# Scores by parity of the head on quarter-size products, one turn of the probabilities per parity, and other duration numbers in the planner of an attention, FFT and feed-forward kernel

## The chip, the cores and the metric

The kernel runs on one core of a Trainium2 chip, in one launch. The metric is device time in microseconds (us), from the first instruction to the last with what lies around them; the median of the runs is compared. Engine names are those of the profile: PE is TensorE (matrix products, with PEld for its weight loads), DVE is VectorE, ACT is ScalarE, POOL is GpSimd, SP is SyncE, whose queue issues the transfers.

## What is computed

Sliding-window attention (8 batches, 8 heads, 576 tokens, head size 64, each query sees itself and the 63 keys before it), whose output is mixed by a two-dimensional FFT, added back, normalized and sent through a two-layer feed-forward network of width 2048.

```python
def _attn_ref(q, k, v):
    scores = scale * np.matmul(q, k.transpose(0, 1, 3, 2))
    mask = (rel >= 0) & (rel < window)            # rel = query - key, window = 64
    scores = np.where(mask, scores, -1000000000.0)
    ...
    return np.matmul(attn, v)

def _moe_ref(x, w_ch1, w_ch2):
    X = np.fft.fft(np.fft.fft(x, axis=1), axis=2)
    u = x + np.real(X)
    un = (u - mu) / np.sqrt(var + 1e-06)
    return u + np.maximum(un @ w_ch1, 0.0) @ w_ch2
```

## The kernel before

**Tiles and stages.** The 4608 tokens are 36 tiles of 128 (T = 0 to 35); two batches make 9 tiles. `attn_tile(T)` loads k, q and v, turns k and q so that the head size lies on the partitions, makes scores, masks and exponentiates them, turns the probabilities, multiplies with v and normalizes into `xu`. `fft(b)` mixes a batch (products `pg`, then `pz`), `norm_tile` adds and normalizes, `ffn(c)` runs the feed-forward network on a chunk of two tiles: for each of 16 slices f twelve products of 256 columns into `ph` (L1207), a relu in two parts (ACT L1222, then DVE L1225) and six products of 512 columns into `po` (L1188). Chunk 0 is done in f32, all others in pairs of f16 parts (high and low), three products for one.

**Two kinds of attention tile.** Tiles below `PRO` = 13 are plain: f32, turned by PE through PSUM and copied out. From 13 on tiles are split: an ACT cast makes the high part, POOL or DVE subtracts it for the low part, and the turn is a transposing DMA on SP's queue: one for k (L487), two for q (L499), four for the probabilities (L626), one for the FFT's input in most tiles (L765), one for the normalized input of the feed-forward network (L1050).

**Scores before.** A tile's 128 queries are worked in two halves of 64, called jj. In a plain tile q is copied by two ACT or DVE copies into a zeroed, block-diagonal layout (`qbd`), so that one 128x128 product (L568) makes the scores of a pair of heads for one half: four products per half, eight per tile. In a split tile a half takes 16 products with 64 columns of weights (L575). Partitions of a score tile `psc` are (parity of the head, 64 queries). Since an output tile `pa` of the product with v (L657) holds four heads for both halves, both of its parts read the turned probabilities of both halves.

**What sets the order.** Nothing runs in the order of the code. Every step is an `op` with an engine (or two to choose from), a duration, a latency, a priority and the buffers it reads and writes; `Plan.order` simulates engines and rings of buffers and emits the instructions in the order found, each engine's queue in that order. PE, DVE, ACT, POOL and SP each work their queue strictly in that order. Feed-forward products have priority numbers over 1e6, so they fill what attention and FFT leave free. An op that may go to two engines goes to the second when that would be done earlier by more than a margin. `SEM` is added to a result that another engine reads, `SELF` to one that the same engine reads, `FIXED` to every duration; `TURN` and `HTURN` are the time that a transposing DMA holds SP's queue. Where the planner sees a gap on PE before the feed-forward network starts, `warm` products fill it.

**Rings.** `pr` (scores and probabilities) and `pt` (turned probabilities) have two buffers, PSUM ring `ps` four, `xu` ten: the first product with v of tile T takes the `xu` buffer that tile T - 10 leaves.

## Time and profile before

| | |
|---|---|
| median of 3 runs | 1018.03 us (1016.69 to 1024.65) |
| span of the profiled execution | 1015.3 us |
| PE busy | 972.7 us, 96% of the span |
| DVE, ACT, POOL busy | 679.6, 417.9, 197.4 us |
| granted TensorE clock, mean | 0.993 |

Busy time is the union of the engine's instructions. Matmuls are pipelined, so a busy PE is not PE at its peak. In rows with a bracket, the bracket holds the idle time before the instruction and what ended it. A queue's own rows (SPq) show how long issuing took, not the transfer.

### The profile page before, as it was taken

The page shows a single profiled execution, that of the slowest core. Times are in us where ns is not written, and L with a number is a line of the kernel's source. Part 1 is how long each engine was busy: PE and PEld are TensorE (multiplying, and loading weights), DVE is VectorE, ACT ScalarE, POOL GpSimd, SP SyncE. Part 2 cuts the span into 40 slices and gives each one's busy share as a digit, 9 for nine tenths or more (in the row PEclk, how much of TensorE's full clock was granted, in tenths as well). Part 3 has the DMA queues.
Part 4 walks back from the last instruction along what each step waited for, and adds up shares of the span by engine and source line. Part 5 has one row for each costly group of instructions (what it writes and reads, how often), then busy time and mean ns, then how long its engine had stood idle before and what let it go on. Part 6 is the DMA issues. An engine that isn't in the chain of part 4 may idle for free.

```text
span 1015.3 us, 22449 instructions
## 1 busy us (share of the span) xinstructions
PE 972.7 (96%) x8756; PEld 687.3 (68%) x8756; DVE 679.6 (67%) x1979; ACT 417.9 (41%) x1047; POOL 197.4 (19%) x203
## 2 busy tenths in 40 slices
PE   8889989999999989998999999999999999999998
PEld 7677757676676657665676666766676667676665
DVE  5899899888777767565787769676686636441121
ACT  6666656744554335323354335333453213121111
POOL 1000100042244223332022302233021300220000
PEclk9999999999999999999999999999999999999999
DMA  8987673235989866878668766867565421230000
GB/s 194 244 224 198 191 188 109 71 78 94 160 152 178 160 114 143 142 137 141 126 111 172 144 126 108 173 131 161 89 111 108 94 38 37 60 74 21 1 22 21
DMA packets 310538, 123.06 MB, mean 121 GB/s; under 512 B 292568, under 2 KB 292696, under 8 KB 310432
## 3 DMA queue, kind: packets, MB, share of 16 engines
q1 hardware_dynamic: 307712, 112.71, 54.8%
q0 software_dynamic: 2720, 8.92, 3.3%
q8 instruction: 69, 1.13, 0.5%
q14 instruction: 37, 0.30, 0.1%
HBM read 54.97 MB, written 14.17 MB: 68 GB/s over the span
## 4 chain that ended last, share of the span: by engine, by line
PE 75%; DVE 8%; DMA 8%; SPq 5%; ACT 2%; issue 2%; POOL 0%; DVEq 0%; ACTq 0%; POOLq 0%
PE ph L1207 30%; PE po L1188 30%; PE pz L924 3%; PE pa L657 3%; DMA pt<-flex 2%; DMA kn<-in_k 2%; PE pg L890 2%; PE psc L568 2%; PE psc L575 2%; SPq L626 2%; SPq L499 1%; DVE y L691 1%; PE pp L606 1%; SPq L427 1%; DVE pr L587 1%
## 5 line engine op out<-in xcount | busy, mean ns | idle before, releaser
L1207 PE MATMUL ph<-uhl,w0s 128*128 128x256 f16 (+1 forms) x3384 | 427.1, 277 | 10.1 <-DVE hh L1225 10.1
L1188 PE MATMUL po<-w1s,hh 128*128 128x512 f16 (+1 forms) x1696 | 428.1, 389 | 0.0
L1207 PEld LDWEIGHTS <-w0s 128*128 128x128 f16 x3264 | 318.0, 98 | 97.6 <-issue 14.5
L1225 DVE SCALAR_TENSOR_TENSOR hh<-ph,hh 128x256 f16<-128x256 f32 x272 | 114.5, 422 | 231.7 <-ACT hh L1222 225.8
L1222 ACT ACTIVATE hh<-ph 128x256 f16<-128x256 f32 x272 | 103.6, 382 | 392.9 <-PE ph L1207 297.1
L1188 PEld LDWEIGHTS <-hh 128*128 128x128 f16 x1632 | 157.0, 98 | 138.8 <-issue 1.9
L595 ACT ACTIVATE pr<-pr,nm 128x128 f32<-128x128 f32 x288 | 90.9, 392 | 13.2 <-DVE nm L587 13.1
L587 DVE CUSTOM_DVE_ANT_0 pr<-psc,mskb 128x128 f32<-128x128 f32 x288 | 65.5, 285 | 15.3 <-PE psc L568 11.3
L1045 POOL TENSOR_TENSOR up<-un,up 128x512 f16<-128x512 f32 x33 | 39.7, 1204 | 75.8 <-ACT up L403 73.1
L620 POOL TENSOR_TENSOR flex<-pr,flex 128x512 f16<-128x512 f32 x23 | 27.4, 1190 | 133.8 <-ACT flex L403 93.5
L1022 POOL TENSOR_TENSOR rs<-mv,mhalf 128x1 f32<-128x1 f32 x36 | 21.0, 584 | 157.9 <-DVE mv L1018 152.2
L484 POOL TENSOR_TENSOR flex<-kn,flex 128x512 f16<-128x512 f32 x19 | 25.0, 1314 | 125.0 <-ACT flex L403 119.3
L998 POOL DMA_INDIRECT mt<-md,gix x34 | 36.5, 1073 | 57.4 <-DMA md<-mp 48.8
L657 PE MATMUL pa<-va,pt 128*64 128x65 f16 (+1 forms) x760 | 39.3, 205 | 7.5 <-DMA pt<-flex 7.5
L657 PE MATMUL pa<-ve,pt 128*64 128x65 f16 (+1 forms) x760 | 39.4, 205 | 0.3 <-DMA ve<-va 0.3
L403 ACT CAST flex<-pr 128x512 f16<-128x512 f32 x39 | 24.0, 615 | 23.5 <-DMA pt<-flex 21.1
L691 DVE TENSOR_TENSOR y<-xu 128x256 f32<-128x256 f32 x68 | 32.1, 512 | 0.6
L669 DVE TENSOR_TENSOR xu<-pa,rc 128x256 f32<-128x256 f32 x72 | 30.6, 425 | 2.6
L568 PE MATMUL psc<-kst,qbd 128*128 128x128 f32 x208 | 28.2, 282 | 3.1 <-ACT qbd L403 1.2
L924 PE MATMUL pz<-g,ds__75 97*96 97x257 f16 (+3 forms) x240 | 29.3, 273 | 1.4 <-DVE g L900 1.4
L657 PEld LDWEIGHTS <-pt 128*64 128x64 f16 x1104 | 20.7, 113 | 14.7 <-DMA pt<-flex 7.9
L495 POOL TENSOR_TENSOR flex<-qn,flex 128x1024 f16<-128x1024 f32 x12 | 26.2, 2187 | 16.3 <-ACT flex L403 14.1
(155 smaller groups left out, 1108.0 us busy)
## 6 DMA issues: line engine op xcount, KB each, us to landing
wd<-in_moe_w_ch SPq DMA_DIRECT2D x20, 512.0 KB
out<-xu SPq DMA_DIRECT2D x36, 256.0 KB
ve<-va SPq DMA_DIRECT2D x67, 130.0 KB
kn<-in_k SPq DMA_DIRECT2D x32, 256.0 KB
qn<-in_q SPq DMA_DIRECT2D x32, 256.0 KB
flex<-in_moe_w_ch SPq DMA_DIRECT2D x12, 512.0 KB
flex<-in_v SPq DMA_DIRECT2D x20, 256.0 KB
md<-mp SPq DMA_DIRECT2D x24, 192.0 KB
```

The lines of the kernel that those rows point to most:

```text
L568: nc.tensor.matmul(p_[:, hp], qw, keys(hp, jj), start=True, stop=True)
L587: nc.vector.tensor_tensor_reduce(out=t["pr", jj][:, hp], in0=t["ps", jj][:, hp], in1=mskb[:, m : m + P], scale=-0.125, scalar=3.0e38, op0= ...
L595: nc.scalar.activation(pr, pr, AF.Exp, bias=t["nm", jj][:, hp : hp + 1], scale=-1.0)
L657: nc.tensor.matmul(pa[64 * jj : 64 * jj + 64, hh], pt[:, sl], v_, start=(x == 0), stop=(x == len(mm) - 1))
L691: eng.tensor_tensor(out=o, in0=p0, in1=p1, op=al)
L924: nc.tensor.matmul(pz[:M, c0:c1], ds_[:NJ, a, c[0] : c[0] + c[1]], t["g", gi][:, b_, c0:c1], start=(x == 0), stop=(x == len(mm) - 1),)
L998: nc.gpsimd.indirect_dma_start(out=mts[T], out_offset=None, in_=mds[pb][0 : HR if n < 4 else 2 * HR], in_offset=bass.IndirectOffsetOnAxis( ...
L1045: eng.tensor_tensor(out=t["up"][:, 1], in0=t["un"], in1=t["up"][:, 0], op=ALU.subtract)
L1188: nc.tensor.matmul(t["po"][i], l_, r_, start=(f == 0 and x == 0), stop=(f == NKF - 1 and x == len(mm) - 1))
L1207: nc.tensor.matmul(ph, l_, r_, start=(x == 0), stop=(x == len(mm) - 1))
L1222: nc.scalar.activation(t["hh", f][:, 0], ph, AF.Relu)
L1225: nc.vector.scalar_tensor_tensor(out=hh[:, 1], in0=ph, scalar=0.0, in1=hh[:, 0], op0=ALU.max, op1=ALU.subtract)
```

## The change

1. **Parity in place of halves.** A score tile now holds the heads of one parity g for all 128 queries of the tile: partitions are (half jj, 64 queries). The mask table grows from 320 to 384 columns (three variants of 128). The four heads of parity g, both halves, need only the turned probabilities of that parity, so each of the two products with v waits for one `pt` tile.
2. **Plain tiles: 64x64 products.** q is copied as it lies (one copy of 128x512 in place of two of 64x512), the zeroing of `qbuf` on POOL goes, and scores are 16 products with 64 rows and 64 columns of weights: rows by parity, columns by half, written to two PSUM banks. One op of 1.6 in the planner (`WSC`) in place of two of 0.95; it takes both `pr` buffers at once.
3. **Split tiles: one turn per parity.** Two transposing DMAs of 128 partitions in place of four of 64. The number and size of the products is as before.
4. **The planner's numbers.** `FIXED` falls to 0 (it was 0.1 on DVE and ACT, 0.06 on POOL), `SEM` and `SELF` rise by as much; `TURN` rises from 1.26 to 1.5 and replaces `HTURN` (1.2) for the probabilities, whose latency goes from 1.8 to 2.2.

```diff
-TURN = 1.26
-HTURN = 1.2
+TURN = 1.5
+WSC = 1.6
-    SEM = {"PE": 0.22, "DVE": 0.06, "ACT": 0.06, "POOL": 0.08, "DMA": 0.0}
+    SEM = {"PE": 0.22, "DVE": 0.16, "ACT": 0.16, "POOL": 0.14, "DMA": 0.0}
-    SELF = {"PE": 0.05, "DVE": 0.02, "ACT": 0.02, "POOL": 0.03, "DMA": 0.0}
-    FIXED = {"PE": 0.0, "DVE": 0.1, "ACT": 0.1, "POOL": 0.06, "DMA": 0.0}
+    SELF = {"PE": 0.05, "DVE": 0.12, "ACT": 0.12, "POOL": 0.09, "DMA": 0.0}
+    FIXED = {"PE": 0.0, "DVE": 0.0, "ACT": 0.0, "POOL": 0.0, "DMA": 0.0}
...
-        op("POOL", 1.0, -498 + i, lambda i=i: nc.gpsimd.memset(qbuf[i], 0.0), writes=[Bq[i]])
...
-            for h in range(2):
-                op("ACT", 0.48, base + 0.6, lambda e, h=h: q_copy(h, e), [bpq], [Bq[i]], alt=("DVE", 0.6), port=False)
+            op("ACT", 0.48, base + 0.6, lambda e: copy(e, q32[i], t["pq"]), [bpq], [Bq[i]], alt=("DVE", 0.6), port=False)
...
-                for hp in range(4 if whole else 0):
-                    qw = qbd32[i][:, hp, jj].rearrange("p h s -> p (h s)")
-                    nc.tensor.matmul(p_[:, hp], qw, keys(hp, jj), start=True, stop=True)
...
+        def score(groups):
+            for g in groups:
+                t["pr", g] = sb([P, 4, P], F32, "pr", f"pr{T}_{g}")
+                t["ps", g] = bank("ps", f"psc{T}_{g}")
+            for hp in range(4):
+                for z in range(1 if whole else 2):
+                    for g in groups:
+                        for jj in range(2):
+                            out = t["ps", g][64 * jj : 64 * jj + 64, hp]
+                            if whole:
+                                rows = slice(64 * g, 64 * g + 64)
+                                nc.tensor.matmul(
+                                    out, q32[i][rows, hp, 64 * jj : 64 * jj + 64], keys(hp, jj, rows), start=True, stop=True
+                                )
...
+        if whole:
+            op("PE", WSC, base + 2, lambda: score((0, 1)), rd, [*bss, *bps])
...
-            op("DMA", HTURN, base + 4.2 + jj, lambda g=p_turn: g(0), [bpp], [bt, bt2], lat=1.8)
-            op("DMA", HTURN, base + 4.3 + jj, lambda g=p_turn: g(1), [bpp], [bt2], lat=1.8)
+            op("DMA", TURN, base + 4.2 + g, p_turn, [bpp], [bt], lat=2.2)
...
-            rd = [*bpt[0], *bpt[1], Bve[i], Bva[i]]
+            rd = [*bpt[g], Bve[i], Bva[i]]
```

**Where instructions move.** On SP's queue around the probabilities of tile 24 (`pt24`), a place in the middle of the program, there stood before (`kst` is the turn of k, `qbd` that of q, `py` that of the FFT's input, `kn` and `flex` from `in_v` are loads):

```order
L487 DMA_TRANSPOSE kst_79<-flex_78 128x8x128
L427 DMA qn28_7349<-in_q 128x8x64
L765 DMA_TRANSPOSE py23_7371<-yp23_7299 128x8x128
L626 DMA_TRANSPOSE pt24_0_7398<-flex_78 128x8x64
L540 DMA ve1_83<-va1_81 64x520
L952 DMA md2_7448<-mp4_1_7336 96x512
L427 DMA flex_78<-in_v 128x8x64
L626 DMA_TRANSPOSE pt24_0_7398<-flex_78 128x8x64
L626 DMA_TRANSPOSE pt24_1_7489<-flex_78 128x8x64
L952 DMA md2_7448<-mp4_2_7357 96x512
L499 DMA_TRANSPOSE qbd1_77<-flex_78 128x16x64
L626 DMA_TRANSPOSE pt24_1_7489<-flex_78 128x8x64
```

and now at the same place:

```order
L482 DMA_TRANSPOSE kst_79<-flex_78 128x8x128
L756 DMA_TRANSPOSE py23_7284<-yp23_7269 128x8x128
L626 DMA_TRANSPOSE pt24_0_7307<-flex_78 128x8x128
L535 DMA ve1_83<-va1_81 64x520
L427 DMA flex_78<-in_v 128x8x64
L943 DMA md2_7385<-mp4_1_7288 96x512
L626 DMA_TRANSPOSE pt24_1_7388<-flex_78 128x8x128
L494 DMA_TRANSPOSE qbd1_77<-flex_78 128x16x64
```

Two of the four issues are gone, and the load of q of tile 28 no longer stands ahead. Over the whole program 92 such transposes become 46; all other transfers keep their number.

On PE the products with v of tile 22 (`pa22`) stood behind the 256-column products of chunk 7, slice 8:

```order
L1207 MATMUL ph7_8_6830<-uhl7_5935,w0s_84 128x256
L657 LDWEIGHTS pt22_0_6770
L657 MATMUL pa22_0_6908<-ve0_82,pt22_0_6770 64x65
L657 LDWEIGHTS pt22_1_6826
L657 MATMUL pa22_0_6908<-va0_80,pt22_1_6826 64x65
```

and their first part stands now behind the 512-column products of chunk 7, slice 0:

```order
L1179 MATMUL po7_1_6885<-w1s_85,hh7_0_6731 128x512
L650 LDWEIGHTS pt22_0_6695
L650 MATMUL pa22_0_6902<-ve0_82,pt22_0_6695 64x65
L650 LDWEIGHTS pt22_0_6695
L650 MATMUL pa22_0_6902<-va0_80,pt22_0_6695 64x65
```

The part reads one `pt` tile now, and stands five and a half slices of the feed-forward network earlier. Counted in 256-column products of that network already issued (a 512-column product as two), the first product with v of a split tile stands 111 earlier in the mean of the 23 tiles, from 216 earlier (tile 32) to 96 later (tile 34).

On POOL the rows from the normalization of tile 10 (`rs10`, `mt` is a gather) to the low part of k of tile 20 were, before (`up` is the low part of a normalized tile, `flex` that of k, q or the probabilities `pr`):

```order
L1022 TENSOR_TENSOR rs10_4289<-mv10_4244,mhalf_70 128x1
L998 DMA mt11_4302<-md1_3878,gix_73 128x512
L484 TENSOR_TENSOR flex_78<-kn19_4210,flex_78 128x8x64
L1022 TENSOR_TENSOR rs11_4402<-mv11_4363,mhalf_70 128x1
L998 DMA mt12_4406<-md1_3878,gix_73 128x512
L1045 TENSOR_TENSOR up10_4409<-un10_4331,up10_4409 128x512
L495 TENSOR_TENSOR flex_78<-qn18_4103,flex_78 128x8x128
L1045 TENSOR_TENSOR up11_4495<-un11_4423,up11_4495 128x512
L1022 TENSOR_TENSOR rs12_4525<-mv12_4491,mhalf_70 128x1
L1045 TENSOR_TENSOR up12_4587<-un12_4529,up12_4587 128x512
L484 TENSOR_TENSOR flex_78<-kn20_4538,flex_78 128x8x64
```

and are now:

```order
L1013 TENSOR_TENSOR rs10_4220<-mv10_4200,mhalf_70 128x1
L989 DMA mt11_4247<-md1_3802,gix_73 128x512
L621 TENSOR_TENSOR flex_78<-pr16_1_3867,flex_78 128x4x128
L1013 TENSOR_TENSOR rs11_4366<-mv11_4310,mhalf_70 128x1
L989 DMA mt12_4373<-md1_3802,gix_73 128x512
L1013 TENSOR_TENSOR rs12_4451<-mv12_4425,mhalf_70 128x1
L1036 TENSOR_TENSOR up12_4530<-un12_4454,up12_4530 128x512
L621 TENSOR_TENSOR flex_78<-pr17_1_4313,flex_78 128x4x128
L479 TENSOR_TENSOR flex_78<-kn20_4608,flex_78 128x8x64
```

The low parts of the normalized tiles 10 and 11 and of q of tile 18 are no longer on POOL's queue. What left POOL runs on DVE. Over the program POOL loses 18 of 33 low parts `up`, 6 of 19 of k, 5 of 12 of q, 4 of 23 of the probabilities, 6 of 7 sums of the FFT's input (L718) and one of its folds; DVE takes all of them, and a net 6 casts and scalings of ACT more.

## Rows read from the trace of the kernel before

**Rows 1.** The answer on cores and clock: span of the profiled execution and mean granted TensorE clock.

```profile
core 0: 1015.3 us, clock 0.993
```

**Rows 2.** The table of stretches, one row for each (us from the start): length, then busy time of each engine with its count of instructions in brackets, granted clock as a share, DMA share and GB/s.

```profile
0.00:86.00 86.00, 73.28 (x716) 59.73 (x717) 68.18 (x259) 55.16 (x143) 7.13 (x20) 0.98 0.90 222
86.00:171.00 85.00, 80.15 (x514) 59.13 (x513) 77.52 (x218) 49.46 (x132) 5.64 (x6) 0.98 0.65 175
171.00:800.00 629.00, 607.78 (x5982) 424.46 (x5980) 458.36 (x1326) 273.37 (x671) 164.35 (x155) 0.99 0.69 129
800.00:1015.30 215.30, 211.48 (x1550) 144.02 (x1548) 75.54 (x181) 39.94 (x103) 20.27 (x22) 1.00 0.15 35
```

**Rows 3.** The timeline of PE near the end, where only the feed-forward network is left: start, duration, engine, line, operation, how many.

```profile
999.63 1.47 PE L1207 MATMUL ph<-uhl,w0s 128*128 128x256 f16 x12
...
1002.24 1.47 PE L1207 MATMUL ph<-uhl,w0s 128*128 128x256 f16 x12
```

**Rows 4.** The list of PE's waits over the whole span: what waited, for what, then total us, times, longest.

```profile
PE ph L1207 <- DVE hh L1225: 10.1, 10, 2.8
PE pa L657 <- DMA pt<-flex: 7.5, 4, 3.8
PE ph L1207 <- DVE wf L1111: 3.7, 1, 3.7
```

**Rows 5.** The timeline of all engines around the longest wait of the start.

```profile
149.16 0.73 DVE L1111 SCALAR_TENSOR_TENSOR wf<-flex,wf 128x512 uint16<-128x512 uint32 x1
...
149.95 0.93 PE L1207 MATMUL ph<-uhl,wf 128*128 128x256 f32 x2 [3.67 <-DVE wf L1111]
```

**Rows 6.** The table of stretches again, for two short ones; the last but two of the columns is the granted clock.

```profile
365.00:370.00 5.00, 4.15 (x55) 2.71 (x56) 4.33 (x12) 1.25 (x2) 3.18 (x2) 0.66 0.33 53
467.00:472.00 5.00, 5.00 (x27) 2.93 (x25) 1.67 (x4) 0.38 (x1) 0.00 (x0) 0.66 0.96 194
```

**Rows 7.** SP's issuing by source line: how many, then shortest, median and longest in ns.

```profile
L626 SPq DMA_TRANSPOSE pt<-flex x92: 1193/1264/2272, 254.4 to 820.9; - x92
...
L487 SPq DMA_TRANSPOSE kst<-flex x23: 1231/1316/2780, 156.3 to 735.2; - x23
```

**Rows 8.** The timeline of all engines around the longest of PE's waits for turned probabilities.

```profile
356.05 2.60 SPq L626 DMA_TRANSPOSE pt<-flex  x2
...
360.06 1.14 SPq L427 DMA_DIRECT2D kn<-in_k  x1
...
361.25 1.32 SPq L626 DMA_TRANSPOSE pt<-flex  x1
...
365.85 0.26 PE L657 MATMUL pa<-va,pt 128*64 128x65 f16 x1 [3.76 <-DMA pt<-flex]
```

**Rows 9.** The timeline of all engines around the longest of PE's waits for the relu.

```profile
458.64 2.12 POOL L495 TENSOR_TENSOR flex<-qn,flex 128x1024 f16<-128x1024 f32 x1 [2.20 <-DVE flex L407]
...
459.22 2.10 DVE L620 TENSOR_TENSOR flex<-pr,flex 128x512 f16<-128x512 f32 x1 [0.67 <-ACT flex L403]
...
466.29 0.42 DVE L1225 SCALAR_TENSOR_TENSOR hh<-ph,hh 128x256 f16<-128x256 f32 x1
...
466.76 1.84 PE L1207 MATMUL ph<-uhl,w0s 128*128 128x256 f16 x12 [2.79 <-DVE hh L1225]
```

**Rows 10.** The groups of DVE by line over the span: busy us, mean ns of one, idle before.

```profile
L691 DVE TENSOR_TENSOR y<-xu 128x256 f32<-128x256 f32 x68 | 32.1, 512 | 0.6
...
L758 DVE SCALAR_TENSOR_TENSOR yp<-y,yp 128x512 f16<-128x512 f32 x17 | 14.9, 877 | 0.3
...
L495 DVE TENSOR_TENSOR flex<-qn,flex 128x1024 f16<-128x1024 f32 x11 | 13.4, 1220 | 1.1 <-DMA py<-yp 0.5 <-ACT flex L403 0.5
```

**Rows 11.** DVE by source line: shortest, median and longest in ns of the same operations and of the low parts of the probabilities.

```profile
L691 DVE TENSOR_TENSOR y<-xu x68: 408/419/1390, 17.1 to 830.3; 128x256 f32<-128x256 f32 x68
...
L758 DVE SCALAR_TENSOR_TENSOR yp<-y,yp x17: 676/683/2496, 294.5 to 814.5; 128x512 f16<-128x512 f32 x17
...
L620 DVE TENSOR_TENSOR flex<-pr,flex x23: 679/691/2097, 252.3 to 792.7; 128x512 f16<-128x512 f32 x23
```

**Rows 12.** The groups of POOL between 171 and 800 us: busy us, mean ns of one.

```profile
L1045 POOL TENSOR_TENSOR up<-un,up 128x512 f16<-128x512 f32 x25 | 30.5, 1222 | 64.4 <-ACT up L403 63.5 <-DVE up L407 0.8
...
L495 POOL TENSOR_TENSOR flex<-qn,flex 128x1024 f16<-128x1024 f32 x12 | 26.2, 2187 | 16.3 <-ACT flex L403 14.1 <-DVE flex L407 2.2
...
L484 POOL TENSOR_TENSOR flex<-kn,flex 128x512 f16<-128x512 f32 x18 | 23.5, 1306 | 102.6 <-ACT flex L403 96.9 <-DVE flex L407 5.5
```

**Rows 13.** The timeline of PE in a plain tile: all scores of a tile, after the last products with v of the tile before (f32; each product leaves two records).

```profile
29.04 0.22 PE L657 MATMUL pa<-ve,pt 128*64 128x65 f32 x1
29.04 0.22 PE L657 MATMUL pa<-va,pt 128*64 128x65 f32 x1
29.10 0.22 PE L657 MATMUL pa<-ve,pt 128*64 128x65 f32 x1
...
29.25 2.05 PE L568 MATMUL psc<-kst,qbd 128*128 128x128 f32 x16
```

**Rows 14.** The timeline of PE, of plain scores after 171 us.

```profile
177.81 1.16 PE L568 MATMUL psc<-kst,qbd 128*128 128x128 f32 x8
...
215.89 1.16 PE L568 MATMUL psc<-kst,qbd 128*128 128x128 f32 x8
```

**Rows 15.** The group of ACT's copies of q in plain tiles over the span.

```profile
L403 ACT COPY qbd<-pq 64x512 f32<-64x512 f32 x23 | 13.3, 578 | 4.6 <-PE pq L464 4.4
```

More of the change, by code (lines that the diff above doesn't have):

```diff
@@ L99, in _constants @@
     )
-    sq = (np.arange(P) % 64)[:, None]
+    sq = np.arange(64)[:, None]
     t = np.arange(64)[None]
     own, old, none = t <= sq, t > sq, t + 0 * sq < 0
-    mask = np.concatenate([np.where(m, 0.0, NEG) for m in (own, old, own, none, own)], axis=1)
+    first, second = (own, old), (old, own)
+    both = [(first, second), ((own, none), second), (first, (none, own))]
+    mask = np.where(np.concatenate([np.block([list(a), list(b)]) for a, b in both], axis=1), 0.0, NEG)
     g = np.arange(2 * S)
@@ L324, in attn_fft_ffn_kernel @@
     mhalf = cp.tile([P, 1], F32, name="mhalf")
-    mskb = cp.tile([P, 320], BF16, name="mskb")
+    mskb = cp.tile([P, 3 * P], BF16, name="mskb")
     unit = cp.tile([P, P], F32, name="unit")
@@ L454, in keys @@
             step = old - own
-            return halves[:, own : old + (1 if step > 0 else -1) : step]
+            return halves[rows, own : old + (1 if step > 0 else -1) : step]
         if whole:
@@ new lines, in attn_tile @@
+        bpt, bss = [], [Buf("ps"), Buf("ps")]
+        m = P * (1 if n == 0 else 2 if n == 4 else 0)
+        rd = [Bq[i], bkT, *([] if n == 0 else [BkT[before]])]
+        def score(groups):
[12 more added lines that the diff above has]
+                                )
+                            else:
+                                h = 2 * hp + g
+                                nc.tensor.matmul(
+                                    out, qbd[i][:, jj, h, 64 * z : 64 * z + 64], keys(h, jj), start=(z == 0), stop=(z == 1)
+                                )
@@ L586, in masked @@
+        bps = [Buf("pr"), Buf("pr")]
+        if whole:
+            op("PE", WSC, base + 2, lambda: score((0, 1)), rd, [*bss, *bps])
+        for g in range(2):
+            bs, bp, bnm, bpp, bt = bss[g], bps[g], Buf(), Buf("ps"), Buf("pt")
+            bpt.append([bt])
+            if not whole:
+                op("PE", 0.52, base + 2 + g, lambda g=g: score((g,)), rd, [bs, bp])
+            def masked(g=g):
+                t["nm", g] = sm.tile([P, 4], F32, tag="nm", name=f"nm{T}_{g}")
                 for hp in range(4):
@@ L628, in attn_tile, with p_hi @@
-            op("ACT", 0.52, base + 4 + jj, p_hi, [bp], [bpp], alt=("DVE", 0.34, lazy))
-            op("POOL", 1.12, base + 4.1 + jj, p_lo, [bp], [bpp], alt=("DVE", 0.6, lazy))
-            bt2 = Buf()
-            bpt[jj] = [bt, bt2]
-            op("DMA", HTURN, base + 4.2 + jj, lambda g=p_turn: g(0), [bpp], [bt, bt2], lat=1.8)
-            op("DMA", HTURN, base + 4.3 + jj, lambda g=p_turn: g(1), [bpp], [bt2], lat=1.8)
+            bpp = Bfl[1 + g]
+            def p_hi(eng, g=g):
+                t["pp", g] = half[:, 1 + g].rearrange("p (a z s) -> p a z s", a=4, z=2)
+                copy(eng, t["pp", g][:, :, 0], t["pr", g])
@@ new lines, in p_lo, with p_turn @@
+            def p_lo(eng, g=g):
+                pp = t["pp", g]
+                eng.tensor_tensor(out=pp[:, :, 1], in0=t["pr", g], in1=pp[:, :, 0], op=ALU.subtract)
+            def p_turn(g=g):
+                t["pt", g] = sb([P, 4, 2, P], F16, "pt", f"pt{T}_{g}")
+                dst = t["pt", g].rearrange("p a z s -> p (a z) s")
+                nc.sync.dma_start_transpose(dst, t["pp", g].rearrange("p a z t -> p (a z t)"))
+            op("ACT", 0.52, base + 4 + g, p_hi, [bp], [bpp], alt=("DVE", 0.34, lazy))
@@ L635, in attn_tile @@
+            op("POOL", 1.12, base + 4.1 + g, p_lo, [bp], [bpp], alt=("DVE", 0.6, lazy))
+            op("DMA", TURN, base + 4.2 + g, p_turn, [bpp], [bt], lat=2.2)
         bx, by = Buf("xu"), Buf("y")
```

107 lines of the change are left out of this document (33 added, 74 removed).

## Prediction

> **What bounds the kernel now.** I read the cores first (span 1015.3 us at clock 0.993 [rows 1]), then the stretches [rows 2], then what PE waited for [rows 4]. The reader is to see four stretches. Up to 86 us, no feed-forward work exists yet; DMA is at 0.90 and PE's 73 busy us hold filler products, so PE doesn't bound. From 86 to 171 the f32 chunk fills PE while DVE is busy 77.5 of 85 us; PE's one long wait there, 3.67 us, ends with a weight conversion on DVE [rows 5]. DVE and the loads behind it set when this stretch ends. From 171 to 800 PE always has a product to run and is idle only where the order puts an instruction too early: 629.0 - 607.8 = 21.2 us. From 800 on it is feed-forward work alone. A slice of that work takes 2.61 us (999.63 to 1002.24 [rows 3]); 17 chunks of 16 make 272 x 2.61 = 710 us, 70% of the span, and the change touches none of it. So the time after 171 us is PE's work plus PE's waits, and a change of order can win back at most the waits: 10.1 us for the relu and 7.5 us for turned probabilities [rows 4], and two drops to the lower clock level, 1.2 GHz, just behind such waits [rows 6]: a share of 0.66 over 5 us means 3.4 us at half speed, 1.7 us lost each time.
>
> My sum is made against the profiled 1015.3 us. The median of the runs, 1018.03, lies 2.7 us above that; I add this at the end.
>
> **Turned probabilities (A).** SP holds 1.26 us for a transpose of 64 partitions and 1.32 us for one of 128 [rows 7]: the price is per issue, not per byte. So two issues gone in each of 23 split tiles free 46 x 1.26 = 58 us of SP, and the last of a tile's issues starts 2 x 1.26 = 2.5 us sooner behind the first. The bytes are the same, so the engines that move them win nothing. In the longest wait two issues went out at 356.05, a turn of q and a load came between, the last followed at 361.25, and PE, which had reached the products, stood until 365.85 [rows 8]. Four such waits make the 7.5 us. Taking 2.5 us off each (3.8, and three that share 3.7) would leave 1.3 us. But the order takes part of this back: the planner knows of the shorter queue and puts the products some 110 feed-forward products earlier, 110 x 2.61 / 24 = 12 us on PE's clock. What speaks for a gain all the same is that its allowances grow: 1.5 + 2.2 us per turn, against 4.6 us from the late issue of rows 8 at a congested place, and the first part waits for one turn instead of four. I take 7.5 to 3.0: **-4.5** (bounds -7.5, and +21 if the waits multiply, see the rivals).
>
> **DVE and POOL (B).** In the longest relu wait a POOL subtraction of 2.12 us and a DVE one of 2.10 us lay on each other [rows 9]. The DVE operation usually takes 0.69 us [rows 11]. The relu's second part came behind it in DVE's queue, after masks and normalization, and PE behind that. The same shows in other two-input operations: medians of 0.42 and 0.68 us against means of 0.51 and 0.88 us [rows 10, 11], an excess of 68 x 0.093 + 17 x 0.194 = 9.6 us on these two groups alone, while POOL works. The change moves 40 operations from POOL to DVE. DVE gains 35 x 0.69 + 5 x 1.22 = 30 us [rows 10, 11], and at most 6 x 0.69 = 4 us for casts from ACT. POOL loses 18 x 1.22 + 6 x 1.31 + 5 x 2.19 [rows 12], with the ten others at 1.2 us some 53 us, two fifths of its subtractions. Long holds of two microseconds become rarer, but DVE goes from 458 to about 490 of 629 us. By the rows, two fifths of an excess that I estimate at 25 us over all groups come back: 10 us against 34 us of new work, so DVE as a whole is busier by some 24 us; only the rare long holds shrink. The Trainium skill (SBUF — State Buffer, section "SBUF: two separate sides") says more: DVE and GpSimd take a shared port pair as an exclusive lock for a whole instruction and the loser blocks. Rows 9 agree; by that rule all 53 us that leave POOL could be holds of DVE that end, the net would be 19 us in DVE's favour, and B would be near its lower bound. Since PE waited for the long holds and not for DVE's total (it has 139 idle us there), I take 10.1 to 5: **-5** (bounds -10 and +10, the doubling of the wait if the new work lands in front of relus).
>
> **The clock (C).** With fewer long waits, one of the two drops after 171 us goes: **-1.7** (bounds -3.4 and +1.7).
>
> **Plain scores (D).** A record of the 128x128 products starts every 0.11 us: 16 records in 1.78 us and the last one's end [rows 13]. A tile now has 32 records of the same columns. Two products on different column halves do run together: records of the products with v start in pairs at the same instant, a pair every 0.06 us [rows 13]. If the four quarters run in pairs, a tile takes 16 x 0.11 = 1.78 us, as before; if all four run at once, 0.89 us; if none do, 3.55 us. No row shows two products on different row halves. The nearest rows are the column pairs, so pairs are sure and four at once open; I take the middle, 1.33 us. The Trainium skill (TensorEngine Tiling (Array Packing), section "Tiling Modes") says that tiles of 64x64 are four independent tiles that load and multiply in parallel; by that rule a tile would take 0.89 us and D would be -1.3. What it is worth depends on the place: before 171 us loads and DVE set the pace and hide it. After it only three half tiles of plain scores are left [rows 14], 1.5 tiles x 0.45: **-0.7** (bounds -1.3 and +2.7). That a tile's scores now take both `pr` buffers at once, so that the next tile's scores wait for both flips, costs nothing while tiles come at the pace of the loads (some eight in the first 86 us, DMA at 0.90 [rows 2]); without this cover it would cost about one group of exponentials per tile.
>
> **The rest (0).** One copy of q in place of two saves 0.58 us in each of 13 tiles [rows 15], and two clearings at the start go: all behind the loads. SP's loads up to the last weight stand in nearly the same order, and DVE's queue up to the f32 chunk's last conversion is as long as before, so I leave 149.95 us where it is (bounds -3 and +4).
>
> **Sum.** -4.5 - 5 - 1.7 - 0.7 = -11.9: a span of 1003.4, and with 2.7 us a time of 1006.1 us.
>
> **Rivals.**
> - *The waits move and nothing is won.* The order is tighter by 12 us, so PE waits elsewhere for as long. For it: the same in-order PE, the same bytes. Only D stays, and one us of B: 1015.3 - 1.7 + 2.7 = 1016.3.
> - *More is won.* All waits of A and B go, both drops, D by four quarters: -7.5 - 10 - 3.4 - 1.3 = -22, 996 us. Against it: some of the waits come from DVE's queue order, which nobody planned to mend.
> - *The products with v stand too early.* The one that ends slower. PE stands still at a split tile's first product until the turn lands; a wait is 7.5 / 4 = 1.9 us. Today 4 of 23 tiles wait. If 15 do, A is 28.5 - 7.5 = +21; with B and D that is +15.3, so 1033 us. With B and D kept, it turns slower by over 1% when about 13 tiles wait. For it: the advance of 12 us, and DMA at 0.69 over the whole stretch, more in bursts. Against it: 58 us less on SP.
> - *The quarters run one after the other.* 3.55 us a tile, 1.78 more. After 171 us +2.7; between 86 and 150 us 3.5 tiles, 6.2 us, of which the 3.7 us wait hides most: +2.5; before 86 us 8 tiles, 14 us, beside 12.7 idle us and filler, half of it hidden at worst: +4 as an estimate. With A, B, C: -2, 1016 us.
>
> **How the numbers follow.** The forecast 0.45 (own range 999 to 1012), no gain 0.22, more gain 0.12, products too early 0.13, quarters in a row 0.08. One per cent, about what a measurement can tell from no change, is 10.2 us: faster means under 1007.9. Of the forecast's 0.45 I put 0.36 below this, all of the larger gain too: 0.48 faster. Slower than 1028.2 is only the order that is too early: 0.13. The rest, 0.39, is the same. The range leaves out the slow rival and the far half of the large gain: 994 to 1021.
>
> **What would show it.** Right: 46 transposes at L626 of about 1.3 us each; PE's waits for `pt` near 3 us and for the relu near 5 us; fewer DVE subtractions over 2 us; plain scores in less than 1.8 us a tile, with 32 records closer than 0.06 us; the first f16 product of chunk 1 still near 171 us. Wrong: waits for `pt` at most of the tiles, relu waits over 15 us because DVE is fuller, 32 records spread over 3 us, or a conversion wait that ends later than 150 us.

## The result and the profile after

The changed kernel takes 1029.33 us (median of 4 runs, 1026.41 to 1030.21), the kernel before 1019.65 in the same session: ratio 1.0102, interval [1.0068, 1.0135]. It is slower by one per cent. The forecast was 1006.1 and the range 994 to 1021: wrong in sign. The profiled execution spans 1028.4 us, 13.1 more than [rows 1], and 13.1 us have to be found. The medians lie only 9.7 us apart: the profiled execution is the slowest of its four, so some 3 us of what follows are scatter between executions.

The answer on cores for the changed kernel:

```profile
core 0: 1028.4 us, clock 0.989
```

Its stretches, with the columns of [rows 2]:

```profile
0.00:86.00 86.00, 68.17 (x819) 50.43 (x819) 62.58 (x247) 48.99 (x129) 6.26 (x19) 0.96 0.88 215
86.00:171.00 85.00, 80.61 (x579) 57.92 (x577) 79.93 (x223) 52.20 (x140) 7.51 (x10) 0.98 0.64 182
171.00:800.00 629.00, 601.55 (x5894) 416.55 (x5893) 485.01 (x1369) 263.18 (x653) 130.16 (x124) 0.99 0.63 129
800.00:1028.40 228.40, 223.28 (x1668) 151.63 (x1666) 81.94 (x188) 41.71 (x107) 8.31 (x10) 1.00 0.15 36
```

Length less PE's busy time is PE's idle time: 17.8, 4.4, 27.5 and 5.1 us, against 12.7, 4.9, 21.2 and 3.8 before. The first f16 product of chunk 1, with which the long stretch begins, stands in PE's timeline of the kernel before at

```profile
170.13 1.04 PE L1207 MATMUL ph<-uhl,w0s 128*128 128x256 f16 x8
```

and now at

```profile
169.73 1.04 PE L1198 MATMUL ph<-uhl,w0s 128*128 128x256 f16 x8
```

So the 13.1 us arise behind 171 us, and the longer idle time up to 86 us costs nothing: PE is busy for as much less there. Behind 171 us PE is idle for 32.6 us in place of 25.0, 7.5 us more, and busy for 824.8 us in place of 819.3, 5.6 us more. Of the latter the clock has some 1.7 us (one more drop, see below); the rest I have not traced. Over the whole span the granted shares would make the clock's cost 11.3 us (1028.4 x 0.011) in place of 7.1 (1015.3 x 0.007); the trace's own clock records, seven drops to half clock in place of five, make it 10.8 in place of 7.6.

PE's waits, with the columns of [rows 4]:

```profile
PE ph L1198 <- DVE hh L1216: 17.3, 15, 2.6
PE pk L464 <- DMA kn<-in_k: 4.9, 4, 2.7
PE py L741 <- DVE y L682: 4.5, 5, 2.0
PE pz L915 <- DVE g L891: 4.2, 5, 1.7
PE pq L464 <- DMA qn<-in_q: 3.5, 2, 2.2
PE pa L650 <- DMA pt<-flex: 2.7, 1, 2.7
PE pg L881 <- DVE nm L588: 1.9, 1, 1.9
```

The turned probabilities are as forecast, 7.5 to 2.7. The relu wait (the row of `ph` and `hh`) grew from 10.1 to 17.3, and PE waits longer for other work of DVE too (`y`, `g`, and the masks `nm`, behind which a product `pg` of the FFT stood). Behind 171 us all its waits on DVE come to 25.6 us, before to 13.7. Where such a wait can come from shows in the timeline of all engines around the one that ends at 385.26 (start, duration, engine):

```profile
380.69 2.44 POOL L490 TENSOR_TENSOR flex<-qn,flex 128x1024 f16<-128x1024 f32 x1
...
381.07 2.48 DVE L830 TENSOR_TENSOR h<-h,yT 128x388 f32<-128x388 f32 x1
...
382.69 0.69 PE L881 MATMUL pg<-dd,hs 128*128 128x63 f16 x12
383.48 0.55 DVE L849 TENSOR_TENSOR hs<-h,hs 128x388 f16<-128x388 f32 x1
...
383.95 0.41 DVE L1216 SCALAR_TENSOR_TENSOR hh<-ph,hh 128x256 f16<-128x256 f32 x1
...
384.28 0.27 DVE L588 CUSTOM_DVE_ANT_0 pr<-psc,mskb 128x128 f32<-128x128 f32 x1
...
385.26 0.95 PE L881 MATMUL pg<-dd,fs 128*128 128x65 f16 x12 [1.88 <-DVE nm L588]
```

A DVE addition whose median is 0.56 us takes 2.48, and ends 0.42 us behind a POOL subtraction (380.69 + 2.44 = 383.13). Its followers and PE are late by the rest. It is the picture of [rows 9], and the change was to make it rarer. The planner knows of this conflict: `Plan.order` keeps a time `port`, and neither a POOL operation nor a DVE operation marked `port`, as this addition is, is planned to start before it, so that on paper the two never overlap. Here they do, from 381.07 to 383.13. I counted it so: for each DVE operation after 171 us, its duration less the lower quartile of its group (same line and operands). The sum, called excess below, is 49.6 us before and 51.5 after, with 8 and 10 operations over 1 us. These groups mix shapes, and 12 to 18 us of the sum are only that: with the shapes kept apart it is some 32 us before and 39 after. POOL lost 45 us of work, and DVE's excess did not fall in this order. Behind waits of PE the clock falls, three times after 171 us (behind the masks at 385.26, behind `g` at 626.21, and behind the one wait for turned probabilities at 684.76), not twice as in [rows 6]:

```profile
385.00:390.00 5.00, 4.74 (x40) 3.76 (x41) 2.93 (x14) 2.29 (x7) 0.00 (x0) 0.66 1.14 128
627.00:632.00 5.00, 5.00 (x28) 4.08 (x27) 4.54 (x24) 2.84 (x13) 0.00 (x0) 0.66 0.68 158
685.00:690.00 5.00, 5.00 (x50) 2.36 (x43) 4.86 (x20) 2.95 (x8) 1.11 (x2) 0.66 0.49 99
```

The plain scores became faster than I had said. PE's timeline of one plain tile:

```profile
13.78 1.10 PE L566 MATMUL psc<-kst,qbd 64*64 64x128 f32 x32
```

32 records in 1.10 us, against 16 in 2.05 [rows 13]: the four quarters run at once. The Trainium skill (TensorEngine Tiling (Array Packing), section "Tiling Modes") says so of 64x64 tiles, and the trace agrees.

### The profile page after: what moved, and what is told of

Same layout as the page of the kernel before. It is cut to its first block, busy times and chain, and to the rows that moved or that the text cites. A ratio compares the mean times of both kernels' runs of the same rounds, so it can differ in the third digit from the quotient of the medians.

```text
span 1028.4 us, 22730 instructions
## 1 busy us (share of the span) xinstructions
PE 973.6 (95%) x8953; PEld 676.5 (66%) x8953; DVE 709.5 (69%) x2025; ACT 406.1 (39%) x1028; POOL 152.2 (15%) x161
## 4 chain that ended last, share of the span: by engine, by line
PE 66%; DVE 21%; DMA 7%; issue 2%; ACT 2%; SPq 1%; POOL 1%; DVEq 0%; ACTq 0%; POOLq 0%
PE ph L1198 28%; PE po L1179 27%; PE pz L915 3%; PE pa L650 2%; PE pg L881 2%; DMA kn<-in_k 2%; DVE pr L588 2%; DVE hh L1216 1%; DMA py<-yp 1%; PE psc L571 1%; DVE y L682 1%; DMA pt<-flex 1%; DVE xu L660 1%; DVE w0s L1155 1%; DMA uhl<-up 1%
## 5 line engine op out<-in xcount | busy, mean ns | idle before, releaser
L1198 PE MATMUL ph<-uhl,w0s 128*128 128x256 f16 (+1 forms) x3384 | 427.5, 277 | 18.0 <-DVE hh L1216 17.3
L650 PE MATMUL pa<-ve,pt 128*64 128x65 f16 (+1 forms) x760 | 44.3, 208 | 2.9 <-DMA pt<-flex 2.7
L650 PE MATMUL pa<-va,pt 128*64 128x65 f16 (+1 forms) x760 | 44.3, 208 | 0.0
L915 PE MATMUL pz<-g,ds__75 97*96 97x257 f16 (+3 forms) x240 | 32.0, 287 | 4.6 <-DVE g L891 4.2
L915 PEld LDWEIGHTS <-ds__75 97*96 97x96 f16 (+1 forms) x240 | 28.4, 130 | 7.2 <-DVE g L891 3.6
L650 PEld LDWEIGHTS <-pt 128*64 128x64 f16 x1104 | 21.1, 111 | 14.8 <-issue 10.9
L403 ACT CAST up<-un 128x512 f16<-128x512 f32 x32 | 19.7, 615 | 24.6 <-DVE un L1017 11.7
L571 PE MATMUL psc<-kst,qbd 128*64 128x128 f16 x736 | 28.2, 223 | 0.4 <-DVE kst L516 0.4
L571 PEld LDWEIGHTS <-qbd 128*64 128x64 f16 x736 | 22.1, 111 | 9.2 <-issue 8.4
L1236 DVE SCALAR_TENSOR_TENSOR xu<-po,osc,xu 128x512 f32<-128x512 f32 x34 | 23.8, 743 | 5.8 <-PE po L1179 5.8
L403 ACT CAST flex<-pr 128x512 f16<-128x512 f32 x35 | 21.5, 616 | 15.5 <-DMA pt<-flex 15.3
```

The source lines that it names most:

```text
L403: nc.scalar.mul(out, in_, scale) if scale is not None else nc.scalar.copy(out, in_)
L571: nc.tensor.matmul(out, qbd[i][:, jj, h, 64 * z : 64 * z + 64], keys(h, jj), start=(z == 0), stop=(z == 1))
L650: nc.tensor.matmul(pa[sl, hp], pt[:, sl], v_, start=(x == 0), stop=(x == len(mm) - 1))
L915: nc.tensor.matmul(pz[:M, c0:c1], ds_[:NJ, a, c[0] : c[0] + c[1]], t["g", gi][:, b_, c0:c1], start=(x == 0), stop=(x == len(mm) - 1),)
L1198: nc.tensor.matmul(ph, l_, r_, start=(x == 0), stop=(x == len(mm) - 1))
```

## The experiments

Below, "relu wait" is PE's wait for `hh`, read in one profiled execution, whose time can lie 5 us off its kernel's median. "Relu delay" is the time from the end of a relu's first part on ACT to the start of its second on DVE, beyond 0.15 us, summed over 272 relus (57.9 us before, 100.9 after). Ratios are to the kernel before on the same chip in the same session.

### Which part costs: numbers, geometry, or a single order

The change has three parts that can be exchanged: the geometry (scores by parity, quarters, one turn), `TURN`, and the tables `SEM`, `SELF`, `FIXED`. Four runs split them.

The changed kernel with the old tables:

```diff
-    SEM = {"PE": 0.22, "DVE": 0.16, "ACT": 0.16, "POOL": 0.14, "DMA": 0.0}
+    SEM = {"PE": 0.22, "DVE": 0.06, "ACT": 0.06, "POOL": 0.08, "DMA": 0.0}
-    SELF = {"PE": 0.05, "DVE": 0.12, "ACT": 0.12, "POOL": 0.09, "DMA": 0.0}
+    SELF = {"PE": 0.05, "DVE": 0.02, "ACT": 0.02, "POOL": 0.03, "DMA": 0.0}
-    FIXED = {"PE": 0.0, "DVE": 0.0, "ACT": 0.0, "POOL": 0.0, "DMA": 0.0}
+    FIXED = {"PE": 0.0, "DVE": 0.1, "ACT": 0.1, "POOL": 0.06, "DMA": 0.0}
```

> The changed kernel with the planner's three tables SEM, SELF and FIXED of before put back (0.06/0.06/0.08, 0.02/0.02/0.03, 0.1/0.1/0.06); scores by parity, 64x64 quarters and TURN 1.5 stay. Theory N (the new numbers send some 40 operations from POOL to DVE and make DVE's queue run behind the plan): POOL keeps 135 tensor operations instead of 100, PE's wait for the relu goes from 17.3 back to about 10 us, DVE's busy time from 171 to 800 us from 485 to about 460 us, and the time falls to 1005 to 1013 us, under before, because the faster plain scores and the shorter wait for turned probabilities are kept. Theory G (the parity of heads costs, since both pr buffers are taken at once and DVE's masks and normalizations come in another order): the relu wait stays near 17 us and the time stays at 1025 to 1032 us. Theory S (any new order lands somewhere within 1% of the old one, whatever it was made for): relu waits anywhere from 7 to 18 us, a time anywhere from 1008 to 1030, and no agreement between the four runs of this call on which part costs.

Measured: 1022.75 us, ratio 1.0049 [1.0021, 1.0078], relu wait 7.1 us.

The same with `TURN` of before as well:

```diff
-TURN = 1.5
+TURN = 1.26
```

> As the run with the three tables put back, and TURN at 1.26 too: the new geometry with the whole table of before. Theory N: within 4 us of the run that keeps TURN 1.5, since TURN is charged to SP's queue and has no part in what DVE is given: 1005 to 1015 us, relu wait about 10 us. Theory T (the larger TURN places turned operands later and is what moved the order): this run is the fast one and the one with TURN 1.5 stays near 1029. Theory S: over 6 us from the run with TURN 1.5, in either direction, though only one number differs by 0.24.

Measured: 1028.29, 1.0089 [1.0060, 1.0119], relu wait 10.9. The kernel before with the new tables (the first diff, read backwards):

> The kernel before with the new SEM, SELF and FIXED alone; geometry and TURN of before. Theory N: slower than before by 10 us or more, 1028 to 1040, with a relu wait of 15 us or more, POOL at 88 tensor operations and DVE's busy time from 171 to 800 us near 490 us. Theory G: within 4 us of before (1016 to 1024), relu wait about 10 us. Theory S: anywhere from 1010 to 1035.

Measured: 1025.98, 1.0075 [1.0044, 1.0105], relu wait 19.6. The changed kernel with `TURN` 1.26 alone (the second diff):

> The changed kernel with TURN at 1.26 instead of 1.5, its new tables kept. Theory N: 1024 to 1034 us, relu wait 15 us or more. Theory T: back to 1019 or below. Theory S: anywhere from 1010 to 1035, with waits that sit on other tiles than in the changed kernel.

Measured: 1021.96, 1.0033 [1.0003, 1.0063], relu wait 13.7. The relu wait follows the tables in all four, as theory N said; the time doesn't: `TURN` 1.5 in place of 1.26 gains 5.5 us with the old tables and loses 7.4 with the new. That is scatter of the order, and its size had to be known. Five runs move a number by 10 ns. First the changed kernel with `TURN = 1.51`:

> The changed kernel with TURN 1.51 instead of 1.5 and nothing else: a number of the planner that moves by 10 ns. It shows how far a new order scatters. Theory S (scatter of the order, some 5 us either way, is as large as what any part does): 1015 to 1035 us, more than 3 us from the changed kernel as likely as not. Theory N (the numbers and engines decide): within 3 us of 1029.

Measured: 1026.21, 1.0084 [1.0053, 1.0115], relu wait 15.9. The other four change `"PE": 0.22` in `SEM` to `0.23`, or `TURN` to `1.27`. The kernel before with the former:

> The kernel before with one number of the planner moved by 10 ns that belongs to no part of the change (the time it reckons from a PE product to who reads it, 0.22 to 0.23). Theory L (the order before is a favourable one, and any new order costs some 7 us, whatever the reason for it; six new orders so far have medians of 1022 to 1029): 1021 to 1030 us. Theory P (the parts of the change cost, above all the lost 0.1 us that the old table added to each DVE operation and that served as slack): within 4 us of before, 1014 to 1022, and the sum of the relu's delays (second part's start behind the first part's end, over 0.15 us) near the 58 us of before.

Measured: 1022.75, 1.0051 [1.0026, 1.0076], relu wait 8.7. With the latter:

> The kernel before with TURN 1.27 instead of 1.26, again 10 ns that mean nothing. Theory L: 1021 to 1030 us. Theory P: 1014 to 1022 us, relu delays near 58 us.

Measured: 1020.80, 1.0022 [0.9989, 1.0055], relu wait 10.5. New geometry with old tables:

> The run with the three tables of before in the changed kernel, with 0.22 to 0.23 us in the time from a PE product to its reader, 10 ns that mean nothing: a second order of the new geometry with the old numbers (the first two have 1022.8 and 1028.3 us; three of the old geometry with the old numbers have 1018.6, 1022.8 and 1020.8). Theory G2 (the geometry costs some 5 us by itself): 1023 to 1029. Theory L2 (the order before is only a good draw): 1018 to 1029, as likely below 1022 as above 1026.

Measured: 1016.81, 0.9978 [0.9958, 0.9998], relu wait 9.0. Old geometry with new tables:

> The kernel before with the new tables, and 0.22 to 0.23 as above: a second order of the old geometry with the new numbers (the first has 1026.0 us). Theory N2 (the new numbers cost some 5 us by themselves, through later relus): 1024 to 1030 us, relu delays over 70 us. Theory L2: 1018 to 1029 us, as likely below 1022 as above 1026.

Measured: 1032.73, 1.0140 [1.0100, 1.0181], relu wait 14.4. The largest of these relu waits, that of the kernel before with the new tables:

```profile
PE ph L1207 <- DVE hh L1225: 19.6, 21, 2.2
```

Now the eleven orders can be averaged:

| ratio to before, in % above 1 | old tables | new tables |
|---|---|---|
| old geometry | 0, 0.51, 0.22 | 0.75, 1.40 |
| new geometry | 0.49, 0.89, -0.22 | 1.02 (the change), 0.33, 0.84 |
| relu wait, us | 7.1 to 10.9, mean 9.4 | 13.7 to 19.6, mean 16.2 |

The rows' means are 0.58 and 0.56%: no cost or gain of the geometry shows, to within some 0.25%. The columns' are 0.32 and 0.87%: the new tables cost 0.55%, 5.6 us, with a standard error of 0.24% from the scatter within the columns (0.4% each). That is just clear of the scatter, and only over both geometries together: it is 0.83% in the old geometry and 0.34% in the new one, the latter about as large as its own standard error. The relu wait is clear, longer in each of the five orders. So of the change's 1.02% some 0.55 are its tables, and the rest lies within the scatter of single orders: the order before is itself 0.32% better than the mean of its column. DVE's holds don't explain the tables' cost: with the shapes kept apart, its mean excess is lower with the new tables, some 30 us against 36. Theory G fell on the relu wait and on the average time. Theory L holds in part: no order of the old geometry and old tables beat the one before.

### Who holds DVE: one order, three divisions of work

To take the scatter out, the changed kernel's order was written out as a table, so that PE's and SP's orders stay row by row, and only the engine of some operations changes:

```diff
-        for o, gap in zip(plan.order(), plan.gaps):
+        for o, fill in frozen(plan, ORDER):
```

In the first, each operation has the engine that it has before (POOL 201 instructions, not 161). By the two tables 116 operations change: 53 go from DVE to POOL and 15 the other way, 28 from DVE to ACT and 20 the other way:

> The changed kernel's order written out as a table, with the engines of before: the operations that the new numbers had moved from POOL to DVE and from ACT to DVE (and the few that went the other way) go back, each at its place in the changed kernel's order. PE's and SP's orders are untouched. Theory M (the moved operations make DVE too full): DVE's busy time from 171 to 800 us falls from 485 to about 460, relu wait about 10 us, the time 1012 to 1020. Theory O (what costs is where operations stand in the queues, not who does them): POOL takes 1.2 to 2.2 us where DVE took 0.69, so what waits for them is later; the time stays at 1025 or rises to 1035, with more holds of DVE by POOL.

Measured: 1040.19, 1.0214 [1.0189, 1.0239]; relu wait 21.7. DVE's busy time from 171 to 800 us falls to 458.6 as theory M said, but the relu wait and the time rise: theory M fell, and theory O has the direction, not the size. The order was planned with these operations on DVE, so the 11 us are the price of going back within this order and not what the move is worth: POOL takes longer for each, and the plan's `port` no longer keeps them apart from DVE's. In the second, DVE does all that it can do of POOL's work, 58 operations (POOL keeps 97 instructions):

> The changed kernel's order written out as a table, and the 58 operations that POOL does in it and DVE could do given to DVE, each at its place; PE's, ACT's and SP's orders are untouched. POOL keeps what only it does. This takes away what stretches DVE's operations (51 us of excess after 171 us, 10 operations by over 1 us) and adds 58 operations of 0.6 to 1.2 us to DVE. Theory H (the holds of DVE by POOL are what the plan doesn't know and what makes relus late): excess near 10 us, relu delays from 101 us to under 70, PE's waits on DVE shorter, 1012 to 1022 us. Theory F (DVE's queue is too full, whoever's fault a single delay is): DVE's busy time stays near 485 us or rises, relu delays 95 us or more, 1027 to 1040 us.

Measured: 1016.79, 0.9968 [0.9937, 0.9999]. The busy times at the head of the page (share of the span, instructions), with the engines of before:

```profile
PE 979.2 (94%) x8953; PEld 677.9 (65%) x8953; DVE 686.6 (66%) x1977; ACT 409.9 (39%) x1036; POOL 197.6 (19%) x201
```

In the changed kernel itself:

```profile
PE 973.6 (95%) x8953; PEld 676.5 (66%) x8953; DVE 709.5 (69%) x2025; ACT 406.1 (39%) x1028; POOL 152.2 (15%) x161
```

Without POOL's 58 operations:

```profile
PE 973.3 (95%) x8953; PEld 676.2 (66%) x8953; DVE 710.5 (70%) x2089; ACT 406.7 (40%) x1028; POOL 65.6 (6%) x97
```

In this order, the less POOL subtracts, the faster: 1040, 1029, 1017. DVE's excess goes 58.1, 51.5, 19.9 us (some 43, 39, 4 with the shapes kept apart), its operations over 1 us too long 14, 10, 0. The last step puts 58 operations on DVE, and DVE is busy for 1.0 us more: what POOL did for it in 86.6 us it paid back in holds. The addition of the timeline above, by source line (shortest, median, longest in ns), in the changed kernel:

```profile
L830 DVE TENSOR_TENSOR h<-h,yT x8: 553/556/2479, 60.4 to 845.4; 128x388 f32<-128x388 f32 x8
```

And without them:

```profile
L830 DVE TENSOR_TENSOR h<-h,yT x8: 553/555/564, 62.3 to 836.6; 128x388 f32<-128x388 f32 x8
```

The Trainium skill (Perfetto Trace Analysis, section "Optimizing Scalar/DVE Operations") warns that moving operations between these two engines "might not help", since they share a port; in this order, leaving them on POOL hurt by 12 us. But theory H had expected a relu delay under 70, and it stayed at 100.4, as theory F said, and so did most of the relu wait:

```profile
PE ph L1198 <- DVE hh L1216: 15.8, 19, 2.2
```

So taking the holds away, with DVE as busy as before, left most of the relu wait standing. Nor is the conflict unknown to the plan, as theory H has it: `port` is there for it, though the plan doesn't see where the chip departs from its times. What went are the longest waits, 2.6 to 2.2 us, those for `y`, `g` and masks, in part or whole, and two of the three clock drops. Does it hold in orders with the old tables? The same move, 97 operations in the order of 1016.81 us, and 96 in the order of the kernel before:

> The fastest order so far of the new geometry (the three tables of before, and 0.23 us from a PE product to its reader; 1016.8 us), written out as a table, with the 97 operations that POOL does in it and DVE could do given to DVE, each at its place. Theory H (POOL's help costs DVE as much time as it saves, and the holds fall where PE waits): DVE's busy time over the span rises by less than 10 us though it takes 97 operations of 0.6 to 1.2 us, its excess after 171 us falls from 53 to about 20, and the time falls by 4 to 12 us to 1005 to 1013. Theory F (97 operations are too many for DVE, 58 were not): DVE's busy time rises by 30 us or more, relu waits grow, 1018 to 1030 us.

> The kernel before, its order written out as a table, with the 96 operations that POOL does in it and DVE could do given to DVE; nothing of the change is in it. Theory H: DVE's busy time rises by less than 10 us, its excess after 171 us falls from 50 to about 20, the relu wait of 2.8 us at 466 us and its clock drop go, 1006 to 1015 us. Theory F: 1020 to 1032 us. If this gains as the changed kernel's order did, the holds are a cost of this kernel in any order, and the change's move of 40 operations was right in itself and lost its gain to where the new order puts PE's work.

Measured: 1016.64, 0.9991 [0.9969, 1.0013], and 1016.85, 0.9983 [0.9957, 1.0009]. The excess falls to 20.0 and 20.2 us as theory H said, DVE's busy time rises by 28 and 32 us as theory F said, and the time moves by less than its interval: both were wrong on it. The holds cost time in the order of the new tables, and none to be measured in two of the old.

### Padding given back

The new tables take 0.1 us off each DVE and ACT operation and 0.06 off POOL's, and add as much to the time until a reader may start. Over the 1,039 DVE operations of the changed order that is 104 us of planned room. Two runs put it back, once and twice:

```diff
-    FIXED = {"PE": 0.0, "DVE": 0.0, "ACT": 0.0, "POOL": 0.0, "DMA": 0.0}
+    FIXED = {"PE": 0.0, "DVE": 0.1, "ACT": 0.1, "POOL": 0.06, "DMA": 0.0}
```

> The changed kernel with FIXED of before alone (0.1 us more for each DVE and ACT operation, 0.06 for POOL) on top of the new SEM and SELF. Theory P: the sum of the relu's delays falls from 101 us to under 75, PE's wait for the relu from 17 to under 10, the time to 1015 to 1023. Theory L: 1020 to 1030 with no tie between padding and time.

Measured: 1028.28, 1.0101 [1.0052, 1.0150]; relu delay 87.3, relu wait 9.0. With 0.2 for DVE:

> The changed kernel with FIXED at 0.2 us for DVE, 0.1 for ACT and 0.06 for POOL: twice the padding on DVE that before had. Theory P: the sum of the relu's delays falls below 60 us and PE's relu wait below 7; POOL takes even more operations, so DVE's busy time falls below 455 us from 171 to 800; the time is 1012 to 1022, unless POOL's slower subtractions make turned operands late. Theory L: 1020 to 1032, as likely above the run with 0.1 as below.

Measured: 1033.92, 1.0147 [1.0103, 1.0191]; relu delay 63.7. PE's waits in the latter:

```profile
PE ph L1198 <- DMA uhl<-up: 11.1, 3, 5.8
PE po L1179 <- DVE w1s L1102: 4.8, 3, 3.2
...
PE ph L1198 <- DVE hh L1216: 2.8, 3, 1.2
```

The room takes the relu wait away, 17.3 to 9.0 to 2.8, and the time doesn't follow: theory P has the relu wait and not the time. With 0.1, PE's idle time behind 171 us falls by 8 us, but PE is busy for 6 us more there, and the work in front of it ran for 13.7 us at half clock from 146.6 us on, the changed kernel's for 3.4 us. With 0.2, PE waits for the turned input of the network (`uhl`), and the first f16 product of chunk 1 starts at 181.44, not 169.73. Padding on top of the raised `SEM` isn't the old table. Which of the three tables costs stays open.

### Late relus put ahead

> The changed kernel with its order written out as a table (every instruction of every engine in the place that the planner gave it), and one edit: 29 of the 272 second relu parts stand ahead, in DVE's queue, of the operations that started on DVE after the relu's first part had ended on ACT. By the trace of the changed kernel these 29 start 40 us too late in all, 16 of them by over 1 us. Nothing else moves; the geometry and the work of each engine stay. Theory R (PE's longer waits for a relu that stands behind other DVE work are what makes the changed kernel slower): the relu wait falls from 17.3 us to under 7, one or two of the three clock drops after 171 us go, and the time falls by 10 to 16 us, to 1013 to 1020. Theory W (the waits move: the operations that are overtaken are late instead, and PE waits for masks, the transform's operands or turned probabilities): the relu wait falls, other waits on DVE grow by as much, and the time stays within 4 us of 1029.

The edit is to the table `ORDER`: 29 rows of DVE moved up. Measured: 1032.94, 1.0161 [1.0128, 1.0193]. The relu delay falls to 84.8, the relu wait is 17.3 us, as much as without the edit: theory R fell, and theory W has the time and not the waits. DVE's timeline ahead of the longest one, which PE ends at 777.91 (3.38 us):

```profile
774.18 0.67 DVE L1004 TENSOR_TENSOR xu<-xu,mt 32x512 f32<-32x512 f32 x1
774.86 0.68 DVE L1001 TENSOR_TENSOR xu<-xu,mt 32x511 f32<-32x511 f32 x1
...
777.37 0.15 DVE L1009 TENSOR_SCALAR mv<-mv 128x1 f32<-128x1 f32 x1
777.44 0.42 DVE L1216 SCALAR_TENSOR_TENSOR hh<-ph,hh 128x256 f16<-128x256 f32 x1
```

The statistics of a tile are one operation of the plan, 3.3 us without a break, and a relu that comes just behind its start waits for all of it. A reordering from one trace's times moved the waits to other relus.

### The parts of the geometry by themselves

Four quarters or two halves in turn, in the changed kernel's order:

```diff
-            for hp in range(4):
-                for z in range(1 if whole else 2):
-                    for g in groups:
+            for g in groups:
+                for hp in range(4):
+                    for z in range(1 if whole else 2):
```

> The changed kernel, and the 32 products of a plain tile's scores issued one row half after the other, 16 and 16, instead of all four quarters in turn. The order and all else stay. If four quarters run at once only when they are issued in turn, a tile's scores go from some 0.95 us back to about 1.8, 13 tiles cost PE 11 us more. Theory D0 (these are hidden behind the loads and only 1.5 tiles after 171 us count): 0 to +3 us against the changed kernel. Theory D1 (the faster scores carry the start): +8 us or more.

Measured: 1029.26, 1.0104 [1.0068, 1.0141], as the changed kernel. A tile's scores, in PE's timeline:

```profile
13.88 1.59 PE L566 MATMUL psc<-kst,qbd 64*64 64x128 f32 x32
```

1.59 us, not 1.10: issued half by half, fewer of them run at once (the prediction's estimate for pairs was 1.78). The 13 tiles cost 6 us more on PE and no time, as theory D0 said. Last, the kernel before in the order and on the engines of the changed one:

> The kernel before (scores by head pairs, 64 queries a half, four turns a split tile, 128x128 plain scores) in the order and on the engines of the changed kernel: each operation stands where its counterpart stands there, the second turn and the second half of the scores right behind the first; where a product with v needs both halves it follows the later one. Theory O (the order costs, the geometry helps a little): 1030 to 1040 us, because SP's queue is longer by 46 issues in an order that was not made for it. Theory G (the geometry costs): back to about 1019 or less.

Measured: 1107.55, 1.0870 [1.0833, 1.0908]. The wait that it adds:

```profile
PE pa L657 <- DMA pt<-flex: 41.8, 31, 5.4
```

31 waits, not one: the new order counts on the 46 issues that are gone from SP. It tells nothing of the geometry in an order of its own.

## Why the prediction was wrong, step by step

- **Turned probabilities (A), -4.5:** right in size, 7.5 to 2.7. The cause was only half right. In the old geometry with the new tables that wait is 0.7 us, and with the old tables and 10 ns more for PE's results 1.2: it belonged to single orders more than to the queue. That the order takes back what SP wins is shown by the 31 waits of the last run.
- **DVE and POOL (B), -5:** this step failed. Its count of work was near: it had DVE at about 490 us from 171 to 800 us, and 485.0 were measured; POOL lost 45 us for 53 forecast. What failed is the inference behind it, "since PE waited for the long holds and not for DVE's total (it has 139 idle us there), I take 10.1 to 5". The relu wait went to 17.3, and the waits on `y`, `g` and masks grew too. Two results stand against it. Without POOL's subtractions and their holds, at 1.0 us more of DVE's busy time, the relu wait is still 15.8 us, with the same relu delay. In the averages the new tables go with fewer holds (some 30 us of excess for 36) and with 6.8 us more of relu wait, in either geometry. And I priced only who does an operation: that the tables also take 0.1 us of room from each DVE operation, I put at nothing. In the averages the tables are the part that costs, 5.6 us of time. Holds have a price as well, 12 us in the order of the changed kernel and nothing in two orders with the old tables. That the missing room makes relus late, and lets the holds show, fits this and is argued, not shown: it rests on one order of the new kind, putting the room back took the relu wait away and not the time, and `SEM`, `SELF` and `FIXED` were never exchanged one by one from an order of before. The Trainium skill (SBUF — State Buffer, "SBUF: two separate sides") would, by the prediction's estimate, at most have had DVE's net fall by 19 us; the trace has DVE 29.9 us busier (679.6 to 709.5).
- **The clock (C), -1.7:** wrong with B: a drop more after 171 us (+1.7), and by the clock records 3.2 us more over the span.
- **Plain scores (D), -0.7:** the tile was mis-sized (1.33 forecast, 1.10 measured), and worth nothing in time, as the run with 1.59 us a tile shows. Up to 86 us PE is busy 5.1 us less and idle 5.1 us more: the loads set the pace there, as the prediction said.
- **The rest (0):** right; 169.73 for 170.13.
- **The rivals:** none was it. The slower one, products with v too early, has one wait where it needed 13. What came is the upper bound of B, +10, which stood in the range of that term and in no case of its own, though "relu waits over 15 us because DVE is fuller" was named as what would show the forecast wrong.
- **The scatter** was missing altogether: 10 ns in a number that means nothing moves a median by 2 to 7 us. A forecast of -12 us from waits of one order could not be surer than that.

## What to carry to other kernels

When a change alters the numbers of a planner, price the room that they leave as well as the work that they move: here shorter durations in the plan went with longer waits of PE for the relu in all five orders, whatever the reason. Before crediting such a change, or blaming it, move a number that means nothing and see how far the time goes; then freeze the order and change one thing. Here no version beat the kernel before by more than some 0.3%.

## What the hardware showed that I had not expected

POOL's two-input operations saved DVE little: 96 of them, 131 us on POOL, make DVE only 32 us busier (679.6 to 711.7), and in the changed order 58 make it 1.0 us busier. And a DVE record is longer than DVE is occupied: the relu's 0.41 us at 383.95 is followed by the next operation 0.33 us later. The Trainium skill (Perfetto Trace Analysis, "Optimizing Scalar/DVE Operations") says that the end of an instruction overlaps with the next. By this pair of records the new tables, which count that end as time to the reader and not as time of the engine, are the truer ones, and the kernel was not faster for it.
